# Two-stage attention and a rational feed-forward on one core: the issue order of the first thirty units taken from a table

## The chip, the cores and the metric

The kernel runs on one core of a Trainium2 chip. The metric is the device time of one execution in microseconds, the median of a few runs; lower is better. A core has five engines that run side by side, each through its own queue in order: PE (matmul), DVE, ACT and POOL (elementwise) and SP (here it only issues DMAs). An engine that waits for an instruction of another holds up everything behind it in its own queue. That is why the order matters.

## The reference

For each of 8 batches and 8 heads, 32 packed queries `p` attend to 576 keys, and the 576 queries `q` then attend to the 32 results. The 4608 x 512 output goes through a feed-forward layer of 2048 hidden columns whose activation is a ratio of polynomials.

```
p_packed = sm_attn(p, k, v)                 # sm_attn: softmax attention, scale 1/sqrt(64)
x = sm_attn(q, p_packed, p_packed)          # then heads side by side: 4608 x 512
h = x @ w_in                                # 512 -> 2048
P = a[0] + a[1]*h + a[2]*h**2 + a[3]*h**3
Q = 1 + |b[0]|*|h| + |b[1]|*h**2
out = (P / (Q + 1e-6)) @ w_out              # 2048 -> 512
```

`w_in` and `w_out` come as float64: the kernel loads their 64-bit words and converts them to float32 itself.

## The kernel before

**Tiling.** The work is cut into 128 units: batch `bb` (8), half of its 576 rows `x` (2), and chunk `c` of 256 hidden columns (8). A unit's `hidden` (L880) makes two `h` tiles of 128 x 288 on PE; ACT makes `Y`, `U` and `sq` from each; DVE multiplies `Y` up twice; POOL adds `sq` to `U`; ACT takes Ln and Exp of `U` into `V` (that is 1/Q); DVE makes two products and the result `gh`, `gl` and `G`. Three units later `acc_block` (L963) multiplies that with `w_out` into the `acc` tiles. Units 0 to 11 are plain: their matmuls take undivided float32 operands. From unit 12 on, operands are split into a high and a low part.

**Work beside the units.** `attention(bb)` (the tiles `kx`, `small`, `ppT`, `nat`, `pn`, `rv`, `AH`, `AL`) makes the attention of one batch in 16 steps during the units of the batch before; `m_chunk` (L852) folds its result with `win` into the `m` tiles. `convert` (L495) turns the 16 weight chunks into float32 while the first units run: two ACT passes, a mask and a shift on DVE (TENSOR_SCALAR, SCALAR_TENSOR_TENSOR), and a final add, on DVE (ISA in the order, CUSTOM_DVE in the profile) and POOL in turn. Its raw words lie in `m` and `w` tiles until then. `divide` (L477) later splits the converted `w_out` chunks, with an ACT cast and two POOL subtractions. `load` and `load_words` issue the DMAs, nearly all from SP.

**What sets the order.** No engine call is issued at once: `Planner` records them all, `edges` finds what depends on what, and `order` (L250) lays them out. There it runs `schedule` (L192), a list scheduler with priced instructions (`COST`, `WAY`, `DMA_RATE`), forwards and backwards for five values of `SLACK` and `ROUNDS` rounds each, and takes the layout with the earliest modelled end. `nc.pin()` (L1011) gives the first loads fixed ranks. `issue` (L281) then emits the instructions in that layout; all carry its line, L291. Where the layout leaves PE idle after the first `acc`, `idle` adds a few small matmuls on a tile of zeros.

Tile names in the order carry their buffer and a running number (`h0_5_156` is the fifth `h` tile, the first of unit 2; `V0_15` belongs to unit 14; `at0_27` and `at1_26` hold the first scores of batch 1).

## Time and profile before

| | |
|---|---|
| median of 3 runs | 777.11 us (776.41 to 777.18) |
| the profiled execution, its own time | 776.27 us |
| its span, first to last instruction | 774.5 us |
| PE / DVE / ACT / POOL busy over the span | 740.3 / 687.1 / 653.0 / 473.2 us |
| mean granted PE clock | 0.99 of full speed |

The shares over the whole span hide that the kernel has stages. Two views show them: the slices of the page, and the sums of busy time over chosen stretches, whose columns are the stretch and its length, then PE, PE's weight loads (PEld), DVE, ACT and POOL, each with its count of instructions as (x...), then the granted PE clock, the busy share of the DMA engines and GB/s. A matmul's end is modelled, so PE can read as busy while it waits; how many matmuls a stretch holds says more than its busy time. The count "idle before <-" behind a row of the timeline is how long that engine stood, and what ended it.

### The profile page before, as it was taken

The numbers are of one execution on the slowest core, as the hardware profiler recorded it, in microseconds if no ns is written. First come the engines' busy times: TensorE is split into PE (matmuls) and PEld (weight loads), VectorE is DVE, ScalarE is ACT, GpSimd is POOL, SyncE is SP. The second block draws the span as 40 slices with busy tenths as digits, with TensorE's granted clock in tenths as the row PEclk, the third lists the DMA queues.
The fourth block names the chain that finished last, engine by engine and source line by source line (L and its number), as shares of the span: only waits on it lengthen the run. The fifth ranks groups of instructions, "written<-read, shape, count | busy, mean of one in ns | idle before, by whom it ended". The sixth has DMA issues, their size and how long they took to land.

```text
span 774.5 us, 14987 instructions
## 1 busy us (share of the span) xinstructions
PE 740.3 (96%) x5332; PEld 568.4 (73%) x5332; DVE 687.1 (89%) x1289; ACT 653.0 (84%) x1465; POOL 473.2 (61%) x456
## 2 busy tenths in 40 slices
PE   2779999999999999999999999999999999999997
PEld 2445554588778887778788887778788887868885
DVE  4899999998999889998999889998999889998863
ACT  5789988999887898889886898989887898898872
POOL 1143568876695557756686556755686556866663
PEclk9879999999999999999999999999999999999999
DMA  9992630204601155023701155023701141000001
GB/s 299 338 372 76 193 41 0 85 29 55 104 1 56 44 68 91 1 87 48 111 1 55 45 55 104 2 86 41 117 1 55 42 57 35 1 2 28 28 0 41
DMA packets 152171, 56.03 MB, mean 72 GB/s; under 512 B 122272, under 2 KB 141472, under 8 KB 152096
## 3 DMA queue, kind: packets, MB, share of 16 engines
q1 hardware_dynamic: 151856, 54.81, 31.0%
q8 instruction: 42, 0.69, 0.4%
q14 instruction: 33, 0.27, 0.1%
q10 hardware_dynamic: 240, 0.26, 0.1%
HBM read 45.62 MB, written 9.44 MB: 71 GB/s over the span
## 4 chain that ended last, share of the span: by engine, by line
PE 68%; DVE 16%; DMA 7%; ACT 4%; issue 2%; POOL 2%; SPq 1%; ACTq 0%; DVEq 0%; POOLq 0%
PE acc L291 35%; PE h L291 20%; PE at L291 12%; DVE Y L291 8%; DMA w<-in_moe_w_in_dram 2%; DMA m<-in_moe_w_in_dram 2%; DVE V L291 2%; DVE kx L291 2%; DVE m L291 2%; DVE small L291 2%; DMA w<-in_q_dram 1%; SPq L291 1%; ACT Y L291 1%; POOL gl L291 1%; DVE w L291 1%
## 5 line engine op out<-in xcount | busy, mean ns | idle before, releaser
L291 POOL TENSOR_TENSOR U<-U,sq 128x576 f32<-128x576 f32 x128 | 185.4, 1449 | 94.6 <-ACT sq L291 47.3
L291 PE MATMUL acc<-w,gh 128*128 128x512 f32 x736 | 235.7, 406 | 0.7 <-DVE G L291 0.4
L291 PE MATMUL h<-AH,m 128*128 128x288 f32 x1024 | 199.5, 317 | 4.0 <-DVE Y L291 3.5
L291 PEld LDWEIGHTS h<-AH,m 128*128 128x128 f32 x1024 | 161.2, 189 | 46.5 <-DVE Y L291 24.5
L291 POOL TENSOR_TENSOR gl<-Y,gh 128x512 fp32r<-128x512 f32 x116 | 150.3, 1296 | 45.0 <-ACT gh L291 22.8
L291 PEld LDWEIGHTS acc<-w,gh 128*128 128x128 f32 x736 | 132.6, 188 | 38.7 <-issue 9.1
L291 ACT ACTIVATE Y<-h,abS 128x288 f32<-128x288 f32 x256 | 127.5, 513 | 30.5 <-PE h L291 26.2
L291 PE MATMUL acc<-w,gl 128*128 128x512 f32 x384 | 149.3, 413 | 0.0
L291 DVE SCALAR_TENSOR_TENSOR Y<-Y,abS,V 128x576 f32<-128x576 f32 x128 | 103.2, 806 | 35.2 <-ACT V L291 34.9
L291 ACT ACTIVATE sq<-h 128x288 f32<-128x288 f32 x256 | 108.4, 425 | 29.0 <-PE h L291 15.7
L291 DVE TENSOR_TENSOR Y<-Y,h 128x288 f32<-128x288 f32 x256 | 111.0, 448 | 20.6 <-ACT U L291 7.6
L291 DVE SCALAR_TENSOR_TENSOR Y<-Y,abS,h 128x288 f32<-128x288 f32 x256 | 125.7, 507 | 2.2
L291 ACT ACTIVATE U<-h 128x288 f32<-128x288 f32 x256 | 101.9, 426 | 8.0 <-DVE V L291 7.0
L291 ACT ACTIVATE V<-U,one 128x576 f32<-128x576 f32 x128 | 98.7, 771 | 8.0 <-DVE Y L291 3.8
L291 DVE SCALAR_TENSOR_TENSOR V<-U,V 128x576 f32<-128x576 f32 x128 | 96.4, 753 | 0.0
L291 PE MATMUL h<-AL,m 128*128 128x288 f32 x448 | 96.3, 295 | 0.0
L291 DVE SCALAR_TENSOR_TENSOR Y<-V,Y 128x576 f32<-128x576 f32 x116 | 87.1, 751 | 1.4
L291 PEld LDWEIGHTS acc<-w,gl 128*128 128x128 f32 x384 | 71.8, 188 | 20.7 <-issue 6.8
L291 ACT ACTIVATE V<-V 128x576 f32<-128x576 f32 x128 | 85.0, 664 | 0.8
L291 ACT CAST gh<-Y 128x512 fp32r<-128x512 f32 x116 | 74.1, 638 | 7.4 <-DVE Y L291 6.9
L291 PE MATMUL acc<-half,gh 128*128 128x512 f32 x240 | 80.0, 411 | 0.0
L291 POOL COPY G<-Y 128x64 f32<-128x64 f32 x116 | 27.5, 237 | 76.7 <-DVE Y L291 70.5
(139 smaller groups left out, 1007.5 us busy)
## 6 DMA issues: line engine op xcount, KB each, us to landing
w<-in_moe_w_out_dram SPq DMA_DIRECT2D x16, 512.0 KB, 6.6
out_dram<-half SPq DMA_DIRECT2D x15, 512.0 KB, 3.0
nat<-in_k_dram SPq DMA_DIRECT2D x48, 144.0 KB, 3.8
nat<-in_q_dram SPq DMA_DIRECT2D x48, 144.0 KB, 4.3
nat<-in_v_dram SPq DMA_DIRECT2D x24, 256.0 KB, 3.4
m<-in_moe_w_in_dram SPq DMA_DIRECT2D x10, 512.0 KB, 6.9
w<-in_moe_w_in_dram SPq DMA_DIRECT2D x6, 512.0 KB, 8.7
nat<-in_k_dram SPq DMA_DIRECT2D x4, 512.0 KB, 6.4
```

Of the source, the lines that this page charges most:

```text
L291: getattr(getattr(self.nc, engine), name)(*args, **kwargs)
```

## The change

`order` no longer schedules. It reads a permutation of all recorded instructions from a string in the source, ORDER, and emits them so. `replay` computes modelled start times for that permutation with the same prices as before; they are used only to place the small idle matmuls. The list scheduler, its slack values, and the pinning of the first loads are gone. What the permutation holds was made elsewhere: the scheduler's order, in which a search moved instructions of the first thirty units.

```diff
+ORDER = (
+    "c-rk)cXV9UnSbAC`n;Jpy-Oo$G?J`l8C>LoZ7ghDD2Bxp6TGw#5&|S_*Z?UcVY4A8gk<4lSwm=ngkmqo#s-WF;3_v<)NE-~W<1jL"
...
-    ROUNDS = 6
-    SLACK = 60, 100, 150, 220, 300
...
-    def schedule(self, before, after, rank, back=0):
...
+    def replay(self, order, before):
+
+        start, end = [0.0] * len(order), [0.0] * len(order)
+        free, port = dict(self.FIRST), {"vector": 0.0, "gpsimd": 0.0}
         mode, landed, dma = None, [], 0.0
...
+        for i in order:
+            e = self.ops[i][0]
+            s = max([free[e]] + [end[j] + self.WAY.get((self.ops[j][0], e), self.PASS) for j in before[i]])
...
+        low, high = np.frombuffer(zlib.decompress(base64.b85decode(ORDER)), np.uint8).reshape(2, -1).astype(int)
+        order = (np.cumsum(low + 256 * high) % 2**16).tolist()
...
+        self.start, self.end = self.replay(order, before)
+        self.deps, self.t0, self.best = dict(enumerate(before)), self.start, (max(self.end), self.start, self.end)
+        return order
...
-    nc.pin()
```

In the built program each engine has the same instructions as before, except that PE has 2 small idle matmuls where it had 10. From about unit 32 on, every engine's order is the same as before. (All rows of the order carry the line of `issue`, L291 before and L314 now.) Up to there most moves are short. Two places follow.

**First place: the scores of batch 1, beside units 0 to 2.** On PE, before: the scores go to `at1_26` and `at0_27`, and the last part of `at0_27` (32x64, over the remainder keys) stands behind the `h` tiles of unit 2.

```order
L291 MATMUL at1_26_173<-kx0_2_143,small_74 32x256
L291 MATMUL at0_27_174<-kx0_2_143,small_74 32x256
L291 MATMUL at1_26_173<-kx0_2_143,small_74 32x256
L291 MATMUL at0_27_174<-kx0_2_143,small_74 32x256
L291 MATMUL h0_5_156<-AH0_3_113,m1_7_135 128x288 x2
L291 MATMUL h1_6_160<-AH0_3_113,m1_7_135 128x288 x2
L291 MATMUL at0_27_174<-kx0_2_143,small_74 32x64 x4
```

On PE, now:

```order
L314 MATMUL at1_26_173<-kx0_2_143,small_74 32x256
L314 MATMUL at0_27_174<-kx0_2_143,small_74 32x256
L314 MATMUL at1_26_173<-kx0_2_143,small_74 32x256
L314 MATMUL at0_27_174<-kx0_2_143,small_74 32x256
L314 MATMUL at0_27_174<-kx0_2_143,small_74 32x64 x4
L314 MATMUL h0_5_156<-AH0_3_113,m1_7_135 128x288 x2
L314 MATMUL h1_6_160<-AH0_3_113,m1_7_135 128x288 x2
```

The remainder part of `at0_27` now stands ahead of the `h` tiles of unit 2.

On ACT at the same place, before (`at0_25` holds the transposed `p` that the scores need, `w5_7` and `m3_6` are raw weights, the `h0_5` rows are unit 2's):

```order
L291 COPY kx0_2_143<-at1_24_164 128x256
L291 COPY small_74<-at0_25_165 128x256
L291 ACTIVATE w5_7_121<-w5_7_121 128x1024
L291 ACTIVATE m3_6_134<-m3_6_134 128x1024
L291 ACTIVATE Y2_3_154<-h0_5_156,abS_68 128x288
L291 ACTIVATE U0_3_152<-h0_5_156 128x288
L291 ACTIVATE half1_2_187<-w5_7_121 128x1024
L291 ACTIVATE sq0_3_155<-h0_5_156 128x288
```

On ACT, now:

```order
L314 COPY kx0_2_143<-at1_24_164 128x256
L314 COPY small_74<-at0_25_165 128x256
L314 ACTIVATE half1_2_187<-w5_7_121 128x1024
L314 ACTIVATE w2_10_163<-w2_10_163 128x1024
L314 ACTIVATE m3_6_134<-m3_6_134 128x1024
L314 ACTIVATE sq0_3_155<-h0_5_156 128x288
L314 ACTIVATE U0_3_152<-h0_5_156 128x288
L314 ACTIVATE Y2_3_154<-h0_5_156,abS_68 128x288
```

The first pass over `w5_7` has gone from here to ten places further up, ahead of unit 1's rows; the first pass over `w2_10` has come in ahead of unit 2's; and unit 2's `Y` comes behind its `sq` and `U` instead of first.

**Second place: loads and conversion of the sixth to eighth weight chunks.** On SP, before (`w3_5`, `w4_6`, `w5_7` are raw weights, `nat1_4` keys and `AH1_2` remainder queries of batch 1):

```order
L291 DMA w2_4_118<-in_moe_w_out_dram 128x512 x2
L291 DMA pn0_2_108<-in_p_dram 32x2x64
L291 DMA nat1_4_112<-in_k_dram 128x4x256
L291 DMA AH1_2_107<-in_q_dram 32x4x128 x2
L291 DMA w3_5_119<-in_moe_w_out_dram 128x512 x2
L291 DMA pn0_2_108<-in_p_dram 32x2x64
L291 DMA w4_6_120<-in_moe_w_in_dram 128x2x256 x2
L291 DMA w5_7_121<-in_moe_w_out_dram 128x512 x2
```

On SP, now:

```order
L314 DMA w2_4_118<-in_moe_w_out_dram 128x512 x2
L314 DMA pn0_2_108<-in_p_dram 32x2x64
L314 DMA w4_6_120<-in_moe_w_in_dram 128x2x256
L314 DMA w3_5_119<-in_moe_w_out_dram 128x512 x2
L314 DMA AH1_2_107<-in_q_dram 32x4x128
L314 DMA w4_6_120<-in_moe_w_in_dram 128x2x256
L314 DMA AH1_2_107<-in_q_dram 32x4x128
L314 DMA nat1_4_112<-in_k_dram 128x4x256
L314 DMA w5_7_121<-in_moe_w_out_dram 128x512 x2
```

Half of `w4_6` and both halves of `w3_5` now go ahead of the keys `nat1_4`, which have moved behind both. Further down the queue (not shown) `w2_10` has likewise gone ahead of the values `nat0_5`, and at its start the first half of batch 0's remainder queries has gone ahead of batch 0's keys and the loads of `b` and `a` ahead of a half each of its queries.

On DVE, where batch 0's attention ends and `w2_4` and `w3_5` are converted, before:

```order
L291 TENSOR_TENSOR kx0_1_87<-kx0_1_87,small_74 128x576
L291 SCALAR_TENSOR_TENSOR w2_4_118<-w2_4_118 128x1024
L291 STREAM_TRANSPOSE AH0_3_113<-kx0_1_87 128x576
L291 TENSOR_SCALAR w3_5_119<-w3_5_119 128x1024
L291 TENSOR_TENSOR Y0_1_127<-Y0_1_127,h0_1_129 128x288
```

On DVE, now:

```order
L314 TENSOR_TENSOR kx0_1_87<-kx0_1_87,small_74 128x576
L314 STREAM_TRANSPOSE AH0_3_113<-kx0_1_87 128x576
L314 SCALAR_TENSOR_TENSOR w2_4_118<-w2_4_118 128x1024
L314 TENSOR_SCALAR w3_5_119<-w3_5_119 128x1024
L314 TENSOR_TENSOR Y0_1_127<-Y0_1_127,h1_2_132 128x288
```

The shift of `w2_4`, behind which POOL's add of `w2_4` may start, now stands behind both transpositions into `AH` and directly ahead of the mask of `w3_5`.

## Rows read from the trace of the kernel before

**Rows 1.** The page, busy tenths in 40 slices of 19.4 us.

```profile
DVE  4899999998999889998999889998999889998863
...
DMA  9992630204601155023701155023701141000001
```

**Rows 2.** Busy sums over stretches: start:end, length, engines (x instructions), clock, DMA, GB/s.

```profile
0.00:30.00 30.00, 12.80 (x171) 10.08 (x172) 16.77 (x27) 18.48 (x29) 5.79 (x9) 0.94 1.01 317
30.00:60.00 30.00, 22.66 (x183) 12.60 (x182) 27.32 (x56) 24.20 (x50) 8.32 (x5) 0.83 1.03 346
60.00:110.00 50.00, 49.34 (x326) 27.01 (x326) 49.23 (x90) 48.94 (x103) 25.37 (x14) 1.00 0.44 112
110.00:150.00 40.00, 39.74 (x207) 20.32 (x206) 39.51 (x76) 33.39 (x72) 33.08 (x27) 1.00 0.08 24
150.00:230.00 80.00, 80.00 (x602) 64.86 (x601) 73.10 (x140) 71.23 (x164) 57.74 (x58) 1.00 0.31 54
230.00:750.00 520.00, 516.23 (x3764) 417.76 (x3763) 470.75 (x888) 447.86 (x1033) 332.96 (x336) 1.00 0.25 47
```

**Rows 3.** Timeline of DVE around 60 us: start, duration, instruction, idle time before.

```profile
59.93 0.49 DVE L291 TENSOR_REDUCE small<-at 128x1 f32<-128x320 f32 x1 [2.12 <-PE at L291]
...
60.57 0.69 DVE L291 TENSOR_SCALAR w<-w 128x1024 int32<-128x1024 int32 x1
61.18 0.45 DVE L291 TENSOR_TENSOR Y<-Y,h 128x288 f32<-128x288 f32 x1
```

**Rows 4.** Timeline of PE, 55 to 60 us.

```profile
55.19 1.11 PE L291 MATMUL at<-kx,small 64*32 64x256 f32 x16 [2.07 <-ACT small L291]
56.22 3.40 PE L291 MATMUL h<-AH,m 128*128 128x288 f32 x8
59.55 0.32 PE L291 MATMUL at<-kx,small 64*32 64x64 f32 x8
```

**Rows 5.** Timeline of ACT, 42 to 59 us.

```profile
42.01 1.14 ACT L291 ACTIVATE w<-w 128x1024 f32<-128x1024 f32 x1 [1.41 <-DMA w<-in_moe_w_out_dram]
...
44.68 1.16 ACT L291 ACTIVATE w<-w 128x1024 f32<-128x1024 f32 x1 [0.44 <-DMA w<-in_moe_w_in_dram]
...
46.69 0.50 ACT L291 ACTIVATE Y<-h,abS 128x288 f32<-128x288 f32 x1
47.08 0.41 ACT L291 ACTIVATE U<-h 128x288 f32<-128x288 f32 x1
...
54.59 0.55 ACT L291 COPY small<-at 128x256 f32<-128x256 f32 x1
54.85 1.35 ACT L291 ACTIVATE w<-w 128x1024 f32<-128x1024 f32 x1
...
58.55 0.50 ACT L291 ACTIVATE Y<-h,abS 128x288 f32<-128x288 f32 x1 [1.32 <-PE h L291]
```

**Rows 6.** The chain that ended last, up to 60 us: start, length, what.

```profile
20.61 9.08 DMA w<-in_q_dram
...
47.98 8.52 DMA w<-in_moe_w_in_dram
```

**Rows 7.** Timelines of POOL and DVE: the same operations, held up and not.

```profile
44.44 2.41 POOL L291 TENSOR_TENSOR w<-w,w 128x1024 int32<-128x1024 int32 x1 [1.89 <-DVE w L291]
...
44.91 2.50 DVE L291 TENSOR_SCALAR w<-w 128x1024 int32<-128x1024 int32 x1
...
83.38 1.21 DVE L291 CUSTOM_DVE_ANT_0 win<-w,win 128x2048 uint16<-128x2048 uint16 x1
...
104.47 2.12 DVE L291 CUSTOM_DVE_ANT_0 w<-w,w 128x2048 uint16<-128x2048 uint16 x1
```

**Rows 8.** What PE's weight loads waited for, 150 to 235 us: total, times, longest.

```profile
PEld h L291 <- DVE Y L291: 1.5, 4, 0.8
PEld at L291 <- POOL half L291: 0.3, 1, 0.3
PEld acc L291 <- ACT gh L291: 0.3, 1, 0.3
```

More of the change, by code (lines that the diff above doesn't have):

```diff
@@ L1 @@
-import heapq
-from collections import deque
+import base64
+import zlib
 from contextlib import ExitStack
@@ L68, in __init__ @@
     def __init__(self, nc):
-        self.nc, self.ops, self.pinned = nc, [], 0
+        self.nc, self.ops = nc, []
     def __getattr__(self, engine):
@@ new lines, in replay @@
+    def replay(self, order, before):
+        start, end = [0.0] * len(order), [0.0] * len(order)
+        free, port = dict(self.FIRST), {"vector": 0.0, "gpsimd": 0.0}
+        mode, landed, dma = None, [], 0.0
+        for i in order:
+            e = self.ops[i][0]
+            s = max([free[e]] + [end[j] + self.WAY.get((self.ops[j][0], e), self.PASS) for j in before[i]])
+            if e == "sync" and len(landed) >= self.IN_FLIGHT:
+                s = max(s, landed[-self.IN_FLIGHT])
+            if e == "tensor" and self.modes[i] != mode:
+                s, mode = s + self.SWITCH, self.modes[i]
+            if self.shared[i]:
+                s = max(s, port["vector" if e == "gpsimd" else "gpsimd"])
+                port[e] = s + self.costs[i]
+            start[i], end[i] = s, s + self.costs[i]
+            free[e] = end[i]
+            if e == "sync":
+                dma = max(dma, s + self.DMA_START) + self.transfers[i]
+                end[i] = dma + self.DMA_END
+                landed.append(end[i])
@@ L256, in order @@
         before = self.edges()
[L257 to L279 removed]
+        low, high = np.frombuffer(zlib.decompress(base64.b85decode(ORDER)), np.uint8).reshape(2, -1).astype(int)
+        order = (np.cumsum(low + 256 * high) % 2**16).tolist()
+        place = {i: r for r, i in enumerate(order)}
+        assert sorted(order) == list(range(n)), "the order is of another program"
+        assert all(place[j] < place[i] for i in range(n) for j in before[i]), "the order breaks a dependence"
+        self.start, self.end = self.replay(order, before)
+        self.deps, self.t0, self.best = dict(enumerate(before)), self.start, (max(self.end), self.start, self.end)
+        return order
     def issue(self, idle):
```

145 lines of the change are left out of this document (71 added, 74 removed).

## The prediction

> **What bounds the kernel now.** I read the slices first [rows 1]: the DMA engines are full for the first three slices, some 60 us, and DVE is at 9 from the third to the ninth. The sums by stretch [rows 2] make stages of this. Up to 60 us the DMA share is 1.01 to 1.03, so the loads set the pace, and DVE is idle for 13.2 + 2.7 us of it. From 60 to 110 us DVE is busy 49.2 of 50 us and ACT 48.9; from 110 to 150 DVE 39.5 of 40 while ACT has 6.6 us to spare. PE reads as busy there too, but holds only 326 matmuls in 50 us and 207 in 40, that is 52 to 65 per 10 us; from 150 us on it holds 72 to 75 per 10 us and DVE falls to 73.1 of 80. So the program has three parts: loads until 60 us, DVE (for a while beside ACT) until 150, PE after that. The order behind unit 32 is unchanged, and PE has no long gap there (516 of 520 us busy). What the change brings is therefore the time by which DVE finishes its head part earlier, plus what PE's stretch from 150 to 230 us gains or loses by its own new order.
>
> **DVE's work in the head does not shrink.** I counted its queue in the two orders up to the product `V0_15` of unit 14, which runs at about 150 us: 250 instructions before, 249 now, one subtraction on 512 columns fewer; on ACT it is 247 and 247. So no large block of work is moved out of the part that DVE bounds. What can go is time in which DVE stands, or is held up: 2.7 us idle between 30 and 60 us, 0.8 between 60 and 110 and 0.5 after that [rows 2], and operations that take longer beside POOL. That is the frame: a few microseconds of 776, not tens.
>
> **Term 1, the gap ahead of 60 us.** DVE stood 2.12 us [rows 3] for a maximum over scores whose last matmuls (0.32 us) stood behind eight `h` matmuls of 3.40 us [rows 4]. Now they stand ahead of those, so this wait goes; the next one is late then. DVE's following operation of unit 2, at 61.18 [rows 3], needs an ACT pass over unit 2's first `h`. I follow that chain. ACT waited 1.41 and 0.44 us for the loads of `w3_5` and `w4_6` [rows 5], which now go earlier, and unit 0's `h`, which ACT needs next, is released 1.21 us earlier, because on DVE the last transposition now stands ahead of one such shift instead of behind it (1.21 us is the length of the byte operation of the same size in [rows 7]). So ACT is 1.85 us ahead at unit 0. It then does one more conversion pass, 1.14 us [rows 5], and ends the copy that the scores wait for at 55.14 - 1.85 + 1.14 = 54.4. The scores and their last part end 0.05 + 1.11 + 0.32 us later, at 55.9. Unit 2's first `h` reached ACT 58.55 - 56.22 = 2.33 us after its start [rows 4, 5], so now at 58.2. ACT meanwhile has three conversion passes, to 57.8, if the load of `w2_10` is there when the second begins, at 55.5. Before, its first half landed at 47.98 + 8.52 = 56.50 [rows 6]; a half is 512 KB, 1.5 us at 346 GB/s [rows 2], so it was whole at 58.0. Now it goes ahead of 512 KB of values: whole at 56.5. So ACT stands 1 us, ends the passes at 58.8, does `sq`, `U` and then `Y` in the new sequence, some 0.3 + 0.3 + 0.5 us [rows 5], and DVE can begin at 59.9 instead of 61.18. I take **-1.3 us**. The ends are 0, if ACT's pass comes no earlier, and -3.9, if all of the 2.12 us goes and with it the 1.81 us by which the mask of `w3_5` was held up (2.50 against 0.69 [rows 3, 7]).
>
> That hold-up is the one place where a page bears on the sum. The row shows the mask starting 0.47 us into POOL's add of 2.41 us and ending only after it [rows 7]. The Trainium skill, SBUF — State Buffer, section "Who interferes with whom", says that DVE in such a mode and POOL lock each other out for a whole instruction and that whichever issues first wins; the row agrees, 1.81 us of it. By that rule the new order, with the mask right behind the shift that releases POOL, gives the lock to DVE and the sum would be up to 1.8 us better, 772.1. I take nothing more for it, because behind the mask DVE waits for ACT's `Y` of unit 0 in either case, and POOL's add then ends later, which is what the first rival is about.
>
> **Term 2, work put off.** At unit 6 (about 100 us) DVE has two instructions fewer in front of it, a byte operation of 1.21 us and a mask of 0.69 [rows 3, 7], 1.9 us together, and ACT two fewer as well; by unit 14 all but the one subtraction has come back. What counts is the state at about 150 us, so I take **-0.7 us**, the price of one operation of that size (the mask of 0.69 is the nearest row), with 0 and -1.9 as ends.
>
> **Term 3, waits and hold-ups between 60 and 150 us.** DVE was idle 1.3 us there in all [rows 2], and at least one byte operation took 2.12 us for 1.21 [rows 7], 0.9 us lost to POOL. Several neighbourhoods of POOL and DVE operations are new, some of POOL's pairs of subtractions are pulled apart. I take one such hold-up less, **-0.9 us**. Ends: -3.1 (all idle time and two hold-ups gone) and +0.9 (one more).
>
> **Term 4, the first loads.** 64 KB of remainder queries now go ahead of batch 0's keys, and 3 KB of `b` and `a` ahead of its last queries. The queue is full, so they cost their bytes: 67 KB at 317 GB/s [rows 2] is **+0.2 us** on the landing that ended at 29.69 [rows 6]. Ends: 0 and +0.4.
>
> **Term 5, units 15 to 32 under PE.** Between 150 and 235 us PE's weight loads waited 2.1 us for other engines [rows 8]. The new order can take some of it or add as much. I take **-0.5 us**, ends -2.1 and +2.1. The eight small idle matmuls that go stood in gaps and cost nothing.
>
> Everything else in the table (the sequence of the two `h` tiles within a unit, of `Y`, `U` and `sq`, of the constants) I cost at nothing. What hides it is that DVE's queue is full; if the cover goes, such a swap costs one ACT pass, 0.3 to 0.5 us.
>
> **The sum.** -1.3 - 0.7 - 0.9 + 0.2 - 0.5 = -3.2 us against the profiled execution's 776.27 (span 774.5 and 1.8 us around it): 773.1. The median of the three runs, 777.11, lies 0.84 above it, so I forecast 773.9, that is 0.4% faster. The terms' ends taken together in the usual way of independent errors give 770.5 to 777. About 0.2%, 1.55 us, is what a measurement here can tell from no change: below 775.6 is faster, above 778.7 slower.
>
> **First rival: the load of `w2_10` comes late, and the gain stays inside the noise.** SP may issue it only when POOL's add has freed its buffer, which ended at 44.44 + 2.41 = 46.85 [rows 7]. If the mask of `w3_5` now goes first, POOL begins after it, at 45.6, and ends at 48.0. The first half then lands 8.52 us later [rows 6], at 56.5, the second at 58.0. ACT stands from 55.5 to 58.0, and with it unit 2's passes, which are queued behind: two passes to 60.3, `Y` at 61.4, DVE at 61.5 against 61.18. Term 1 is +0.3 then. With term 3 at nothing the sum is -0.7: 775.6, or 776.4 by the median. For it speaks that ACT waited for a load twice in just this stretch [rows 5]; against it, that the loads ahead of it in the queue are fewer now. It decides from a landing after about 57 us.
>
> **Second rival, slower: DVE behind POOL.** POOL's new order runs a subtraction, two conversion adds and unit 6's add of `U` one after another (one add is 2.41 us [rows 7]) where they stood apart, in the middle of the stretch in which DVE has no slack. Each DVE operation that shares the lock and comes second loses up to 1.8 us, as the mask did. Two more than before eat up the forecast; with three, 5.4 us, term 3 is +5.4 instead of -0.9: 776.27 - 1.3 - 0.7 + 5.4 + 0.2 - 0.5 = 779.4, by the median 780.2. For it speaks that such hold-ups are there already [rows 7]; against it, that POOL is busy only 25 of 50 us in that stretch [rows 2].
>
> **Third rival: both DVE and PE gain near their ends.** Terms 1, 3 and 5 at -2.6, -2.5 and -1.7 give -7.3 with the rest: 769.0, by the median 769.8. That the table does not do what it says I rule out: the order shows it.
>
> **How the numbers follow.** Forecast 0.54, first rival 0.24, second 0.16, third 0.06. Faster is the forecast nearly whole (0.53) and the third, 0.59; the first rival and the forecast's rest make 0.25 for no change; the second 0.16 for slower. The range reaches from the third rival's 769.8 to 779.2, which leaves out the upper two thirds of the second rival, half of the third and little else.
>
> **What would show it.** Right: no DVE wait of 2 us for PE ahead of 60 us, DVE's first operation of unit 2 at about 60 instead of 61.2, the product of unit 14 about 3 us earlier than about 150, and the same distance from there to the end but for half a microsecond. The first rival shows as an ACT wait for a load of over 2 us between 55 and 59 us. The second shows as DVE rows of 2 us and more between 80 and 150 us beside POOL's. I am wrong if unit 14 comes earlier by what I say and the end does not, for then PE's stretch is not what it seems; or if the head gains far more than DVE's idle time and hold-ups hold.

## The result and the profile after

The changed kernel is slower by a quarter of a per cent: 777.64 us against 775.95 us, medians of 22 runs each, ratio 1.0025 (95% interval 1.0015 to 1.0035). A second set of runs gave 777.46 against 775.49, ratio 1.0028 (1.0016 to 1.0040). The time lies inside the range of 769.8 to 779.2, but on the other side of no change than the forecast: the sum was -3.2 us, measured are +1.7 and +2.0. (The forecast started from the median of three runs, 777.11 us; 22 runs of the same kernel gave 775.95.) The profiled execution of the changed kernel took 778.18 us, with a span of 776.3 us.

The busy sums over the same stretches as in [rows 2], with the same columns, now read:

```profile
0.00:30.00 30.00, 12.99 (x173) 10.57 (x173) 14.62 (x34) 18.21 (x30) 6.16 (x9) 0.94 1.01 313
30.00:60.00 30.00, 18.76 (x173) 11.58 (x170) 24.51 (x45) 23.14 (x48) 9.06 (x6) 0.77 0.87 301
60.00:110.00 50.00, 49.69 (x330) 26.92 (x338) 48.34 (x93) 48.12 (x103) 20.34 (x13) 1.00 0.52 142
110.00:150.00 40.00, 40.00 (x204) 20.53 (x202) 38.59 (x78) 35.39 (x75) 33.34 (x27) 1.00 0.02 5
150.00:230.00 80.00, 79.62 (x598) 63.30 (x597) 74.30 (x140) 70.22 (x163) 56.44 (x58) 1.00 0.35 64
230.00:750.00 520.00, 515.92 (x3756) 417.81 (x3755) 469.55 (x884) 446.56 (x1031) 333.22 (x336) 1.00 0.26 47
```

Only the second row differs much. Between 30 and 60 us DVE did 45 instructions instead of 56, the DMA share fell from 1.03 to 0.87, and the granted clock of PE from 0.83 to 0.77. The DMA share is a matter of this one execution: in a second one (after_again, below) it was 1.01, and unit 2 was late all the same.

Where DVE stands is best followed by one instruction of each unit, the product that updates `V`. These are its rows for units 2, 14 and 31, first before:

```profile
70.92 0.76 DVE L291 SCALAR_TENSOR_TENSOR V<-U,V 128x576 f32<-128x576 f32 x1
...
152.00 0.76 DVE L291 SCALAR_TENSOR_TENSOR V<-U,V 128x576 f32<-128x576 f32 x1
...
244.56 0.75 DVE L291 SCALAR_TENSOR_TENSOR V<-U,V 128x576 f32<-128x576 f32 x1
```

and after:

```profile
73.17 0.76 DVE L314 SCALAR_TENSOR_TENSOR V<-U,V 128x576 f32<-128x576 f32 x1
...
151.48 0.76 DVE L314 SCALAR_TENSOR_TENSOR V<-U,V 128x576 f32<-128x576 f32 x1
...
244.90 0.75 DVE L314 SCALAR_TENSOR_TENSOR V<-U,V 128x576 f32<-128x576 f32 x1
```

The changed order is 2.25 us late at unit 2, 0.52 ahead at unit 14 and 0.34 late at unit 31. So it loses 2.25 us ahead of unit 2, gains 2.8 between units 2 and 14, as DVE's stretch should, and gives 0.9 back behind unit 14. The other 1.4 of the 1.8 us by which this execution ends later are lost at about 695 us (first experiment).

Ahead of unit 2, the timeline of DVE (as in [rows 3]) shows that the wait of 2.12 us for the scores is gone, and two others in its place:

```profile
46.24 1.96 DVE L314 TENSOR_SCALAR w<-w 128x1024 int32<-128x1024 int32 x1 [1.14 <-ACT half L314]
50.36 0.46 DVE L314 TENSOR_TENSOR Y<-Y,h 128x288 f32<-128x288 f32 x1 [2.17 <-ACT sq L314]
...
57.89 0.82 DVE L314 TENSOR_TENSOR Y<-Y,h 128x288 f32<-128x288 f32 x2 [1.60 <-ACT Y L314]
...
60.44 0.48 DVE L314 TENSOR_REDUCE small<-at 128x1 f32<-128x320 f32 x1
...
63.10 0.45 DVE L314 TENSOR_TENSOR Y<-Y,h 128x288 f32<-128x288 f32 x1
```

The last row is DVE's first operation of unit 2, at 63.10 instead of 61.18 [rows 3]. The bracket of the second row names `sq`, not `Y`: the planner lets DVE read an `h` tile in PSUM only behind everything that ACT reads from that tile (`turn` in `edges`). The timeline of ACT (compare [rows 5]):

```profile
41.25 1.13 ACT L314 ACTIVATE w<-w 128x1024 f32<-128x1024 f32 x1 [1.34 <-DMA w<-in_moe_w_out_dram]
...
43.98 1.21 ACT L314 ACTIVATE w<-w 128x1024 f32<-128x1024 f32 x1 [1.08 <-DMA w<-in_moe_w_out_dram]
...
49.13 0.90 ACT L314 ACTIVATE Y<-h,abS 128x288 f32<-128x288 f32 x2
49.91 0.42 ACT L314 ACTIVATE sq<-h 128x288 f32<-128x288 f32 x1
...
51.99 1.22 ACT L314 ACTIVATE w<-w 128x1024 f32<-128x1024 f32 x1
...
55.40 0.71 ACT L314 ACTIVATE U<-h 128x288 f32<-128x288 f32 x2 [0.69 <-PE h L314]
...
58.55 0.42 ACT L314 COPY small<-at 128x256 f32<-128x256 f32 x1
...
59.90 1.15 ACT L314 ACTIVATE w<-w 128x1024 f32<-128x1024 f32 x1
```

ACT still waited 1.34 and 1.08 us for loads. Before, it took `Y`, `U` and `sq` of one `h` tile and then of the other (the first two are in [rows 5]), so that DVE could begin with the first; now it goes to and fro between the two tiles of unit 0, and the tile that DVE wants is free only behind the `sq` that ends at 50.33. The copy that the scores need comes at 58.55 instead of 54.59. The timeline of PE (compare [rows 4]) holds the rest:

```profile
37.21 1.01 PE L314 MATMUL at<-win,ppT 64*32 64x256 f32 x16 [2.06 <-ACT m L314]
...
42.69 1.97 PE L314 MATMUL at<-ident,nat 128*128 128x128 f32 x8 [2.23 <-ACT m L314]
44.45 3.69 PE L314 MATMUL h<-AH,m 128*128 128x288 f32 x8
...
50.65 1.62 PE L314 MATMUL at<-ident,nat 128*128 128x128 f32 x8 [1.92 <-ACT m L314]
52.06 3.30 PE L314 MATMUL h<-AH,m 128*128 128x288 f32 x8
...
59.02 0.78 PE L314 MATMUL at<-kx,small 64*32 64x256 f32 x24 [3.00 <-ACT small L314]
59.92 1.24 PE L314 MATMUL h<-AH,m 128*128 128x288 f32 x4
```

Eight `h` matmuls took 3.69 and 3.30 us for units 0 and 1, and PE waited 1.9 to 3.0 us in front of them and of the scores. At full clock, four of them take 1.24 us (last row). So PE stands longer, and what it then does runs partly at the lower of its two clock levels (1.2 instead of 2.4 GHz, a granted clock of 0.50).

### The profile page after: what moved, and what is told of

The parts are those of the page before. It is cut to its first block, busy times and chain, and to the rows that moved or that the text cites. A ratio compares the mean times of both kernels' runs of the same rounds, so it can differ in the third digit from the quotient of the medians.

```text
span 776.3 us, 14959 instructions
## 1 busy us (share of the span) xinstructions
PE 738.5 (95%) x5316; PEld 568.1 (73%) x5316; DVE 681.9 (88%) x1289; ACT 652.3 (84%) x1465; POOL 469.0 (60%) x456
## 4 chain that ended last, share of the span: by engine, by line
PE 80%; ACT 6%; DVE 5%; DMA 4%; POOL 1%; issue 1%; SPq 1%; ACTq 0%; DVEq 0%; POOLq 0%
PE acc L314 41%; PE h L314 25%; PE at L314 14%; DVE Y L314 3%; DMA w<-in_moe_w_out_dram 2%; ACT Y L314 1%; DMA nat<-in_k_dram 1%; DMA m<-in_moe_w_in_dram 1%; ACT V L314 1%; DVE m L314 1%; ACT U L314 1%; ACT sq L314 1%; SPq L314 1%; POOL gl L314 1%; DVE kx L314 1%
## 5 line engine op out<-in xcount | busy, mean ns | idle before, releaser
L314 POOL TENSOR_TENSOR U<-U,sq 128x576 f32<-128x576 f32 x128 | 183.6, 1434 | 98.3 <-ACT sq L314 50.2
L314 PE MATMUL acc<-w,gh 128*128 128x512 f32 x736 | 238.0, 406 | 0.7 <-ACT half L314 0.3
L314 PE MATMUL h<-AH,m 128*128 128x288 f32 x1024 | 204.5, 318 | 3.9 <-DVE Y L314 3.8
L314 PEld LDWEIGHTS h<-AH,m 128*128 128x128 f32 x1024 | 163.8, 191 | 43.0 <-DVE Y L314 21.3
L314 POOL TENSOR_TENSOR gl<-Y,gh 128x512 fp32r<-128x512 f32 x116 | 150.2, 1295 | 49.9 <-ACT gh L314 23.2
L314 PEld LDWEIGHTS acc<-w,gh 128*128 128x128 f32 x736 | 133.1, 189 | 38.0 <-issue 8.1
L314 ACT ACTIVATE Y<-h,abS 128x288 f32<-128x288 f32 x256 | 127.4, 512 | 30.9 <-PE h L314 26.4
L314 PE MATMUL acc<-w,gl 128*128 128x512 f32 x384 | 150.1, 413 | 0.0
L314 ACT ACTIVATE sq<-h 128x288 f32<-128x288 f32 x256 | 107.4, 421 | 32.3 <-PE h L314 17.8
L314 DVE TENSOR_TENSOR Y<-Y,h 128x288 f32<-128x288 f32 x256 | 111.4, 448 | 25.6 <-ACT sq L314 9.0
L314 DVE SCALAR_TENSOR_TENSOR Y<-Y,abS,V 128x576 f32<-128x576 f32 x128 | 103.3, 807 | 34.4 <-ACT V L314 33.8
L314 DVE SCALAR_TENSOR_TENSOR Y<-Y,abS,h 128x288 f32<-128x288 f32 x256 | 126.1, 507 | 2.7
L314 ACT ACTIVATE U<-h 128x288 f32<-128x288 f32 x256 | 102.2, 424 | 8.6 <-DVE V L314 4.2
L314 ACT ACTIVATE V<-U,one 128x576 f32<-128x576 f32 x128 | 98.8, 772 | 5.8 <-DVE Y L314 3.5
L314 PE MATMUL h<-AL,m 128*128 128x288 f32 x448 | 97.8, 296 | 0.0
L314 DVE SCALAR_TENSOR_TENSOR V<-U,V 128x576 f32<-128x576 f32 x128 | 96.5, 754 | 0.0
L314 DVE SCALAR_TENSOR_TENSOR Y<-V,Y 128x576 f32<-128x576 f32 x116 | 87.2, 752 | 1.5
L314 PEld LDWEIGHTS acc<-w,gl 128*128 128x128 f32 x384 | 71.9, 188 | 22.0 <-issue 8.9
L314 ACT ACTIVATE V<-V 128x576 f32<-128x576 f32 x128 | 84.5, 660 | 1.1
L314 PE MATMUL acc<-half,gh 128*128 128x512 f32 x240 | 81.1, 412 | 0.0
L314 ACT CAST gh<-Y 128x512 fp32r<-128x512 f32 x116 | 74.0, 638 | 6.9 <-DVE Y L314 4.1
L314 PEld LDWEIGHTS h<-AL,m 128*128 128x128 f32 x448 | 73.2, 189 | 1.1
```

Of the source, the lines that this page charges most:

```text
L314: getattr(getattr(self.nc, engine), name)(*args, **kwargs)
```

## Experiments

The experiments ran in five sets, each on another chip and beside the kernel before, whose medians were 775.49, 774.66, 776.34, 775.30 and 776.13 us. So ratios are compared, and microseconds only within a set. "Half clock" is the time between 20 and 70 us at the lower clock level, twice the sum of (1 - granted clock) over stretches of 1 us. "PE waits" adds up PE's waits of over 0.15 us from 33 to 62 us. The columns for units 2, 14 and 31 give how much later (+) their product on DVE ends than in the first trace of before; they are of one execution each and hold the pace of its loads too. In the traces of after_m and after_busy_dve the first loads were late: ACT's pass that starts at 12.71 us in after_busy starts at 14.85 in after_busy_dve. The last column says whether the clock fell behind a wait at 695 us, which the first experiment is about.

| kernel | ratio to before (95%) | PE waits, us | half clock, us | unit 2 | unit 14 | unit 31 | low at 695 |
|---|---|---|---|---|---|---|---|
| before, first trace | | 7.3 | 14 | 0 | 0 | 0 | no |
| before_table | 0.9985 (0.9972 to 0.9998) | 8.2 | 7 | -2.6 | -2.6 | -2.7 | no |
| before_fill | 1.0004 (0.9990 to 1.0017) | 7.2 | 14 | -0.6 | -0.6 | -0.6 | no |
| after, first trace | 1.0025 (1.0015 to 1.0035) | 11.1 | 17 | +2.3 | -0.5 | +0.3 | yes |
| after_again | 1.0028 (1.0016 to 1.0040) | 11.7 | 17 | +1.4 | -1.4 | -0.5 | no |
| after_fill | 1.0004 (0.9987 to 1.0020) | 10.2 | 24 | +3.9 | +1.2 | +2.0 | no |
| before_busy | 1.0007 (0.9992 to 1.0023) | 3.7 | 3 | -1.9 | -1.9 | -1.8 | yes |
| after_busy | 0.9990 (0.9973 to 1.0007) | 5.0 | 3 | -2.1 | -4.8 | -3.9 | no |
| before_act74 | 1.0163 (1.0138 to 1.0187) | 9.2 | 27 | +10.0 | +10.0 | +10.0 | no |
| after_act74 | 1.0056 (1.0036 to 1.0075) | 8.4 | 17 | +3.0 | +0.3 | +1.2 | yes |
| before_m | 1.0021 (1.0004 to 1.0038) | 10.3 | 17 | +3.0 | +3.0 | +3.0 | no |
| after_m | 1.0031 (1.0016 to 1.0045) | 10.3 | 20 | +4.4 | +1.6 | +2.5 | yes |
| mix_abb | 1.0002 (0.9986 to 1.0019) | 8.8 | 14 | +0.6 | +0.6 | +0.6 | no |
| mix_bab | 1.0024 (1.0004 to 1.0044) | 9.4 | 20 | +3.4 | +3.4 | +3.3 | yes |
| mix_bba | 0.9993 (0.9976 to 1.0011) | 6.2 | 14 | +0.1 | -2.7 | -2.0 | yes |
| mix_aab | 1.0043 (1.0026 to 1.0059) | 10.7 | 17 | +2.2 | +2.2 | +2.1 | no |
| after_yfirst | 1.0016 (1.0002 to 1.0031) | 10.1 | 14 | +1.2 | -1.6 | -0.9 | yes |
| before_busy_dve | 0.9988 (0.9973 to 1.0003) | 3.7 | 3 | -1.4 | -1.4 | -1.5 | no |
| after_busy_dve | 0.9961 (0.9946 to 0.9975) | 4.5 | 3 | +0.1 | -2.7 | -1.8 | no |
| mix_bba_busy_dve | 0.9973 (0.9958 to 0.9987) | 4.8 | 3 | +0.2 | -2.5 | -1.9 | no |

### Is the loss made at 695 us or in the head?

In the first trace of the changed kernel, PE's single long wait late in the program was followed by slow matmuls. Before, then after, on PE:

```profile
694.97 0.79 PE L291 MATMUL h<-AH,m 128*128 128x288 f32 x4 [1.81 <-DVE Y L291]
```

```profile
695.63 0.90 PE L314 MATMUL h<-AH,m 128*128 128x288 f32 x4 [2.05 <-DVE Y L314]
...
696.81 1.17 PE L314 MATMUL h<-AH,m 128*128 128x288 f32 x4
```

Theory A made this the cause, theory B the head. Both orders ran a second time (`before_table` holds before's order written as a table, instruction for instruction the same program), and each with this edit, which puts twelve small matmuls on zeros ahead of the last accumulation in front of the wait:

```diff
+    FILL = 6078
...
+        if i == FILL:
+            n = 12
-        if nc.start[i] < IDLE_END and n > 0:
+        if (nc.start[i] < IDLE_END or i == FILL) and n > 0:
```

Expected of the repetition of the changed kernel:

> The changed kernel once more, unchanged, for a second trace. Theory A (the end): the head comes out about even (in the first trace unit 31's product is 0.35 us later than before) and the loss is made at about 695 us, where PE stands 2.05 us for DVE and the matmuls behind it run at a granted clock of 0.83 over 10 us. Then this trace shows the head within 0.5 us of the first one and, where the span is 776 us again, the low clock behind 695 us again. Theory B (the head): the head itself varies from execution to execution and is on average 1.5 to 2 us late. Then the product of unit 31 is late by 1.5 us or more here, and the clock behind 695 us need not fall. Time by both: 777.6, ratio 1.002 to 1.003.

Of before's order as a table:

> The order of the kernel before, written as a table and replayed; every queue holds the same instructions in the same order, with the ten idle matmuls. By both theories the time of the kernel before, ratio 0.999 to 1.001; a ratio of 1.002 would say that something other than the order differs. Its trace is the second one of the order before: by theory A the stretch behind 695 us holds the full clock in it, or where it does not, this execution is 1.4 us longer than the first one; by theory B the milestones of the head differ from the first trace's by a microsecond or more.

Of the two filled kernels:

> The changed kernel with twelve small matmuls on zeros (64x256) put into PE's queue ahead of the last accumulation before the wait at 695 us, so that PE works through most of that wait; nothing else moves. Theory A: the matmuls behind the wait keep the full clock, the stretch 690 to 700 us shows 1.00 in place of 0.83, and the time falls by 1.2 to 1.5 us to about 776.2, ratio to before 1.000 to 1.001. Theory B: the clock is a bystander, the time stays at 777.3 to 777.8, ratio 1.002 to 1.003.

> The order of the kernel before with the same twelve matmuls at the same place. Theory A: its first trace holds the full clock behind that wait, so it gains less than the changed kernel does, 0 to 0.7 us, ratio 0.999 to 1.000, and the distance between the two filled kernels is 0.3 to 0.8 us in place of 1.9. Theory B: both gain alike, or neither, and the distance between the two filled kernels stays 1.5 to 2 us.

The second trace of the changed kernel has the full clock at 695 us. Its unit 31 is 0.8 us earlier than in the first trace, where theory A had said within 0.5 us, and 0.5 us ahead of before's, where theory B had said 1.5 us late. The sums from 690 to 700 us of the first and of the second trace:

```profile
690.00:700.00 10.00, 7.95 (x49) 6.09 (x48) 9.00 (x17) 9.43 (x23) 6.01 (x7) 0.83 0.14 52
```

```profile
690.00:700.00 10.00, 7.94 (x56) 6.45 (x43) 9.27 (x17) 9.93 (x24) 6.40 (x8) 1.00 0.14 52
```

Over all traces with a wait of 1.7 us or more there, the clock fell in 7 of 15, with either order, and each time the end came 1.1 to 1.6 us later, against the first trace of before, than unit 100 had been. Where the wait was filled or shortened (five traces) it never fell. So it comes and goes, with either order: in 2 of 8 traces with before's order behind unit 2 and in 5 of 7 with the changed one, which is too few to call a difference. After_fill reads 1.0004, 0.0024 below after_again (1.9 us, give or take 1.6), and the medians of the two filled kernels lie 0.1 us apart. By the times, theory A's forecasts came in for the changed kernel, and theory B's did not. But theory A can't be the whole: unit 2 is 1.4 to 3.9 us late in all three traces of the changed order, long before 695 us, and latest in that of after_fill (an execution of 778.23 us, 2.3 above that kernel's median). So some of the loss is made at 695 us and some in the head.

The head does vary, in both orders, and with it the clock. The sums from 30 to 60 us of before_table and of after_again:

```profile
30.00:60.00 30.00, 21.72 (x183) 12.42 (x183) 29.37 (x58) 26.15 (x56) 8.38 (x6) 0.94 1.02 347
```

```profile
30.00:60.00 30.00, 18.25 (x171) 11.17 (x170) 24.64 (x46) 24.07 (x47) 9.32 (x6) 0.76 1.01 347
```

The same program as before, with a clock of 0.94 instead of 0.83, is at unit 2 2.6 us earlier, and stays so to the end. Some 1.6 us of this is the clock: the scores and the eight `h` matmuls behind them take from 55.19 to 59.62 us before [rows 4], and in before_table only from 54.14 to 56.95, the `h` matmuls 2.21 us instead of 3.40:

```profile
54.74 2.21 PE L310 MATMUL h<-AH,m 128*128 128x288 f32 x8
```

The other 1.0 us is there on ACT at 42 us already, behind a load that landed 1.0 us earlier.

A trace is one execution, but every execution has its mean granted clock, and this gives its time at half clock over the whole span (1 to 3 us at the very end included). On average it is 13.0 to 14.0 us for before (five sets), 21.7 and 20.3 for the changed kernel, and 17.3 for after_fill. So PE spends about 8 us more at the lower level with the changed order, and not only in the traces shown. Over the 22 executions of the changed kernel, each microsecond more of it goes with some 0.3 us more of time (correlation 0.74).

The repetition also says how far to trust a ratio: one program against itself gave 0.9985.

### Holding the clock in the head

Theory B2 takes the clock of the head for the cause. The edit puts 26 small matmuls into PE's waits, into an accumulator that is not in use yet; no other queue changes (in before's order the fourth group stands at 289 instead of 291):

```diff
+    BUSY = {221: 4, 239: 4, 249: 5, 291: 5, 338: 8}
...
+        if i in BUSY:
+            out = next(c[0][1][0] for _, c in nc.ops if ... tensor.name == "acc1_14_172")
+            todo = [("matmul", (out[0:D, 0:P], zero.bitcast(F32), ident), dict(start=True, stop=True))] * BUSY[i]
```

> The changed kernel with 26 small matmuls (64x128 on zeros, into an accumulator tile not yet in use) put into PE's queue ahead of the instructions for which PE waits in the head: 4 and 4 ahead of the second and third chunk of m, 5 and 5 ahead of the two transpositions of the queries, 8 ahead of batch 1's scores. Theory B2 (the clock in the head): with PE at work in its waits the granted clock of 36 to 60 us, 0.72 to 0.75 in three traces of this order, rises to 0.85 or more, the eight h matmuls of units 0 and 1 take 2.2 us in place of 3.3 to 3.7, and the time falls by 1 to 2 us to 775.6 to 776.6, ratio 1.000 to 1.0015. Theory A2: the waits for ACT set the pace there and not the clock; PE's matmuls get shorter but wait for the same copies, the time falls by under 0.6 us, ratio 1.002 or more. If the filling lengthens PE's queue instead, the time rises by up to 1 us.

> The order of before with the same 26 small matmuls at the same instructions. Theory B2: its head had a granted clock of 0.83 and 0.94 in two traces over 30 to 60 us, so it can gain less: 0 to 1.2 us, ratio 0.9985 to 1.000, and its trace shows 0.90 or more over that stretch. Theory A2: no change within 0.5 us, ratio 0.9995 to 1.0005.

The changed order now takes 774.36 us against 774.66 for before. The ratio falls from 1.0028 to 0.9990, that is 2.9 us, give or take 1.6. PE's timeline of after_busy, against the one above (the `zero` row is the filling):

```profile
48.73 2.11 PE L311 MATMUL h<-AH,m 128*128 128x288 f32 x8
...
51.42 1.96 PE L308 MATMUL acc<-ident,zero 128*64 128x128 f32 x16
54.69 0.78 PE L311 MATMUL at<-kx,small 64*32 64x256 f32 x24 [1.31 <-ACT small L311]
```

Unit 1's eight `h` matmuls take 2.11 us instead of 3.30, the scores start at 54.69 instead of 59.02. The sums from 30 to 60 us of after_busy and of before_busy:

```profile
30.00:60.00 30.00, 24.91 (x230) 16.39 (x229) 26.00 (x49) 25.96 (x53) 9.35 (x6) 0.94 1.02 350
```

```profile
30.00:60.00 30.00, 26.27 (x241) 16.88 (x241) 29.15 (x60) 25.96 (x54) 8.60 (x5) 1.00 1.06 349
```

Nothing but PE's idle time was touched, so these 2.9 us were the clock's: theory B2 holds for the changed order. Theory A2 had allowed 0.6. Over all executions the time at half clock fell to 7.9 us. For before's order B2 had forecast 0.9985 to 1.000, and it gained nothing that could be measured by the same filling (1.0007), although its time at half clock fell as well, from 13.3 us to 6.4; in its trace the head is 1.9 us ahead at unit 2, and 1.5 us of that is lost again at 695 us. So a microsecond at half clock costs the changed order more than it costs before's; why is not shown.

The change also took out eight of the ten small idle matmuls. They are not the cause: in the trace of before all ten stand between 66 and 119 us, where the granted clock is 1.00 with either order, and mix_aab (below), which has all ten, is 2.2 us late at unit 2 like the changed kernel.

### Which instructions make PE stand longer?

Theory A2 looked to ACT's order alone. First, all but two of ACT's first 74 instructions were exchanged between the orders. An excerpt (the changed kernel, 33 to 37 us):

```diff
-ACTIVATE w2_4_118<-w2_4_118 128x1024
-COPY m0_5_122<-at0_13_124 128x256
 COPY m0_5_122<-at1_12_123 128x256
+COPY m0_5_122<-at0_13_124 128x256
+ACTIVATE w2_4_118<-w2_4_118 128x1024
```

> The changed kernel, but ACT's first 74 instructions (all up to the copy of the small tile for batch 1's scores, some 55 to 59 us) in the sequence of before, except for two one-column steps of the constants that stay early because DVE's new order needs them. The other queues stay as changed. Theory A2 (ACT's order in the head): in the changed kernel, conversion passes that wait for loads stand ahead of the copies of the m tiles, and the U and sq steps of units 0 and 1 ahead of Y, so PE waits 2.1 to 3.8 us for m at 37 us, 2.2 for m at 42, 3.0 for small at 56 to 59, and DVE 2.2 to 2.9 us for Y at 49. With the old sequence these go back to below 2.1 us and the time falls by 1.3 to 2 us to 775.5 to 776.2, ratio 0.999 to 1.001. Theory C (the clock by chance, whatever the order): the granted clock of the head falls in some executions and not in others, ACT's sequence has no say in it, and the time stays at 777 to 777.6, ratio 1.002 to 1.003.

> The reverse: the kernel before with ACT's same 72 instructions in the changed sequence. Theory A2: it takes on the waits of the changed kernel, without what the other queues gain by their new order: 1.5 to 3 us slower than before, 777 to 778.5, ratio 1.002 to 1.004. Theory C: no change, ratio 0.999 to 1.001.

Both came out slower than what they started from. The exchange reached back to the first loads, where the raw chunks `m0` and `m1` change places on ACT but not on DVE and SP, and batch 0's attention itself was late by about 3 us. So these two say nothing on the place in question, only that ACT's order is tied to the other queues. The next pair exchanged thirteen instructions, from 33 to 45 us:

> The changed kernel, but thirteen ACT instructions between 33 and 45 us (the copies of the m chunks 0 to 2, two exponentials of batch 0 and the conversion passes of w2_4, w3_5 and w4_6) in the sequence of before, copies ahead of passes; all else as changed. This cuts the swap of 74 down to the place where the changed kernel's PE waits begin. Theory D (the trigger is here): the waits of PE for m ahead of the second and third chunk and the transposition, 5.1 to 6.0 us together in the changed kernel, come back to the 2.7 to 4.4 us of before, the granted clock of 36 to 60 us rises from 0.74 to 0.85 or more, and the time falls by 1 to 2 us to 775.6 to 776.6, ratio 1.000 to 1.0015. Theory E (the trigger is elsewhere, in the Y, U and sq sequence of units 0 and 1 or in PE's own order): no change, 777 to 777.8, ratio 1.002 to 1.003.

> The kernel before with the same thirteen ACT instructions in the changed sequence, passes ahead of copies. Theory D: PE's waits for m grow by 1.5 to 3 us, the clock of 36 to 60 us falls below 0.8, and the time rises by 1 to 3 us, ratio 1.0015 to 1.004. Theory E: ratio 0.999 to 1.001.

Before's order suffers by it as theory D says (1.0021, PE's waits from 7.3 to 10.3 us, half clock 17 us). But giving the changed order before's sequence there didn't help (1.0031), although its waits ahead of the second and third chunk of `m` and the transposition fell to 0.50, 1.21 and 2.24 us. Theory D is not the answer for the changed kernel; in its trace PE's chain was already 1.3 us later at 36 us (its first loads were late), and the clock fell for longer (20 us).

So I cut all five queues at two points where both orders have issued the same set of instructions, and took each third whole: up to unit 0's `h` (some 42 us), to unit 2's `h` and the scores of batch 1 (some 58 us), and the rest. The letters name the thirds: a is the changed order, b before's.

> Before's order, except that on all five queues the first third (all up to the h matmuls of unit 0, some 42 us) has the changed order; the small idle matmuls as before. Theory F (the loss is made here, by the m copies behind conversion passes and the new load order): PE waits for m as in the changed kernel, the half-clock time between 20 and 70 us goes to 8.5 us or more, and the time rises by 1.5 to 3 us, ratio 1.002 to 1.004. Theory G (it is made in the second third): ratio 0.999 to 1.001.

> Before's order, except that the second third (from unit 0's h to unit 2's h and the scores of batch 1, some 42 to 58 us) has the changed order. Theory G (Y behind U and sq on ACT, the small copy late, one conversion pass more ahead of it): PE waits 3 us for small and DVE 2 us and more for Y, the time rises by 1 to 2 us, ratio 1.001 to 1.003. Theory F: ratio 0.998 to 1.0005, the latter if the tail of the scores ahead of unit 2's h gains its 2 us wait on DVE.

> Before's order up to unit 2's h and the scores (some 58 us) and the changed order from there on. Theory H (the gain lies here: at a held clock the changed order gets ahead between units 2 and 14 by some 3 us and keeps 1.4): the head keeps before's clock, and the time falls by 1 to 2 us, ratio 0.9975 to 0.999. If the gain lay in the first two thirds, ratio 0.9995 to 1.0015.

> The complement: the changed order up to some 58 us, before's from there on. Theory H with either F or G: it takes the loss without the gain, 1 to 2 us slower than the changed kernel, ratio to before 1.003 to 1.005. If the gain lay in the first two thirds, it is as the changed kernel or faster, ratio 1.001 to 1.0025.

Theory F falls and G's place holds: the first third alone costs nothing that can be measured (1.0002), the second carries the loss (1.0024, and 1.0043 with the first). The intervals of the two thirds alone overlap; what is clear of them is the second third on top of the first, 1.0043 against 1.0002. The time at half clock, averaged over all executions, points the same way: 14.5 us in mix_abb, 15.3 in mix_bba, 17.7 in mix_bab, 19.6 in mix_aab. The last third is where the order gains, as theory H says: 2.7 to 2.8 us from unit 2 to 14 wherever it is in (after, after_again, after_fill, after_busy, mix_bba), nothing where it is not. Of this mix_bba shows only 0.9993 in its time; its trace has one of the falls at 695 us. Mix_bab has DVE's wait for ACT and PE's for the small copy in before's surroundings:

```profile
49.20 0.46 DVE L310 TENSOR_TENSOR Y<-Y,h 128x288 f32<-128x288 f32 x1 [1.94 <-ACT sq L310]
```

```profile
57.85 1.32 PE L310 MATMUL at<-kx,small 64*32 64x256 f32 x24 [3.00 <-ACT small L310]
```

Half clock takes 20 us in its trace (an execution of 780.89 us, 3.3 above that kernel's median), 14 in those of mix_abb and mix_bba. The last test gave ACT a sequence of its own in that third, `Y` first, the pass of `w5_7` behind the small copy:

```diff
-ACTIVATE sq0_1_128<-h0_1_129 128x288
-ACTIVATE U0_1_125<-h0_1_129 128x288
-ACTIVATE U0_1_125<-h1_2_132 128x288
-COPY m1_7_135<-at0_21_151 128x256
 ACTIVATE Y0_1_127<-h1_2_132,abS_68 128x288
 ACTIVATE Y0_1_127<-h0_1_129,abS_68 128x288
...
+COPY m1_7_135<-at0_21_151 128x256
...
-ACTIVATE w5_7_121<-w5_7_121 128x1024
...
+ACTIVATE w5_7_121<-w5_7_121 128x1024
```

> The changed kernel, with the 24 ACT instructions of the second third (units 0 and 1 and the copies beside them) in a new sequence that follows the changed order's own h tiles: Y of both h tiles first, then U and sq, and the pass of w5_7 behind the small copy. Theory G (Y last and the extra pass are the cause): DVE's waits for Y, 2.2 to 2.9 and 1.6 us, fall below 1 us, PE's wait for small from 3.0 to 3.2 us to about 2.0, the half-clock loss over 20 to 70 us from 8.5 us to 7 or less, and the time falls by 1 to 2 us to 775.5 to 776.5, ratio 1.000 to 1.0015. If the loss hangs on PE's or DVE's own new order there, the time stays within 0.6 us of the changed kernel, ratio 1.002 to 1.003.

The ratio of 1.0016 can't be told from the changed kernel's 1.0025. PE's wait for the small copy fell from 3.0 to 2.25 us, but DVE's wait did not fall (2.17 and 2.92 us in the first two traces of the changed kernel), and the time at half clock over all executions stayed at 19.9 us. Its row on DVE:

```profile
48.61 0.45 DVE L311 TENSOR_TENSOR Y<-Y,h 128x288 f32<-128x288 f32 x1 [3.09 <-ACT sq L311]
```

and ACT's at that place:

```profile
46.79 0.89 ACT L311 ACTIVATE Y<-h,abS 128x288 f32<-128x288 f32 x2 [1.82 <-PE h L311]
47.57 0.71 ACT L311 ACTIVATE U<-h 128x288 f32<-128x288 f32 x2
48.15 0.73 ACT L311 ACTIVATE sq<-h 128x288 f32<-128x288 f32 x2
```

`Y` was there at about 47.3 and DVE began at 48.61, right behind the first `sq`. So theory G named the wrong thing: what counts is when the third reader of one tile is done, and my sequence went to and fro between the tiles just like the changed one. A sequence that finishes one tile first, as before's does, was not tried in the changed order. That this is the main cause in the second third is read from the rows and not shown by a run.

### The version that beats both

PE's wait at 695 us comes from DVE: two subtractions for an `m` chunk stand between the products on the `h` tile that PE waits for. They were moved behind:

```diff
-TENSOR_TENSOR m3_37_1402<-at0_195_1403,m3_37_1402 128x512
...
-TENSOR_TENSOR m3_37_1402<-at1_196_1404,m3_37_1402 128x512
...
+TENSOR_TENSOR m3_37_1402<-at0_195_1403,m3_37_1402 128x512
+TENSOR_TENSOR m3_37_1402<-at1_196_1404,m3_37_1402 128x512
```

> The changed order with the 26 small matmuls in the head, and on DVE two subtractions of an m chunk that stand at 692 us between the products of two units moved behind the four products on the h tiles, of which the first releases the h tile that PE waits for 1.8 to 2.05 us at 695 us. Both remaining stretches of half clock (head, and behind 695 us) should be gone: granted clock 0.996 or more, the wait at 695 us 0.6 to 1.0 us, the time 0.8 to 1.8 us below the same kernel without the move: 772.6 to 773.6, ratio 0.9965 to 0.998. If the wait at 695 us is kept by another engine, the time stays at 774.4.

> The order of before with the same two edits, the 26 matmuls and the two subtractions moved. With the clock held in both, the distance to its partner is what the new order is worth by itself. Theory B2 says 1.3 to 2.1 us (at unit 31 the filled traces stand 1.3 to 2.1 us apart): this kernel 774.2 to 775.4, ratio 0.9985 to 1.0. If the new order is worth nothing, the two agree within 0.5 us.

> What helped, joined: before's order up to some 58 us, the changed order from there on, the 26 small matmuls in PE's waits of the head and the two subtractions on DVE moved at 692 us. If the gain of the last third and the held clock add up: as fast as the changed order with both edits or up to 1 us faster, 772.8 to 774, ratio 0.995 to 0.9975. If the second third of the changed order is worth something by itself once the clock is held, this one is slower than that: 774 to 775, ratio 0.9975 to 0.999.

In after_busy_dve the wait is down to

```profile
692.58 0.80 PE L311 MATMUL h<-AH,m 128*128 128x288 f32 x4 [1.12 <-DVE Y L311]
```

and the time is 773.79 us, ratio 0.9961 (0.9946 to 0.9975): faster than both kernels. With the clock held at both places, the changed order is worth 773.79 against 775.23, 1.4 us in its favour. Taking before's first two thirds instead brought nothing more (774.08, ratio 0.9973): once the clock is held, no cost of the second third is left that could be measured.

The ratios side by side:

| | nothing filled | filled at 695 us | filled in the head | filled in the head, wait at 695 us cut |
|---|---|---|---|---|
| before's order | 1 (its copy 0.9985) | 1.0004 | 1.0007 | 0.9988 |
| the changed order | 1.0025 and 1.0028 | 1.0004 | 0.9990 | 0.9961 |

In the changed order either edit takes off about as much as the whole loss, and both together more. In before's order none of the edits is clear of the noise.

## Why the prediction was wrong

**The step that failed is term 1.** It follows a chain of ACT and PE instructions to DVE's first operation of unit 2 at 59.9; it came at 63.10. Three links broke. ACT's waits for loads did not go: 1.34 and 1.08 us instead of 1.41 and 0.44 [rows 5]. The sequence of `Y`, `U` and `sq`, which I costed at nothing because DVE's queue would cover it, was not covered: DVE waited 2.17 and 1.60 us, since ACT finished neither tile early. And I kept the duration of every PE group. The signs were in the rows: [rows 2] has a granted clock of 0.83 for 30 to 60 us and 1.00 behind, and eight `h` matmuls take 3.40 us [rows 4], where after_busy needs 2.11. I read PE as an engine that waits there anyway, and didn't ask what longer waits do to the pace of what follows. The sum had no term for the clock.

The hold-up of the mask of `w3_5`, which I took nothing for, went both ways. In the first trace the mask stood 1.14 us for ACT's second pass, POOL's add had begun at 45.23, and it took 1.96 us (first row of DVE above). In after_again it came right behind the shift, 0.2 us ahead of POOL's add:

```profile
45.38 0.69 DVE L314 TENSOR_SCALAR w<-w 128x1024 int32<-128x1024 int32 x1
```

It brought nothing, for the reason I gave: DVE then waited for ACT, 2.92 us.

**What it should have held.** At unit 2 the three unfilled traces of before's whole order stand at 0, -2.6 and -0.6 us, those of the changed order at 2.3, 1.4 and 3.9. The means differ by 3.6 us against the change. With PE kept busy (two traces each) they differ by 0.7: by -0.2 in one set and by +1.6 in the other, where the changed order's first loads were late. So, as an estimate from ten traces that lie up to 2.6 us apart within one order, the clock takes about 2.9 of the 3.6 us, and the new waits by themselves 0.7, where I had -1.3.

**Terms 2 and 3 were right in kind and too small.** Together I had -1.6 from unit 2 to 14; it was -2.7 to -2.8 in every trace with this part of the order. In the first traces DVE's busy time there fell by 4.5 us (79.85 to 75.36), and its idle time grew from 1.2 to 3.0 us. DVE has 143 instructions there instead of 145. Four held-up byte operations of 1.53, 1.64, 2.12 and 2.12 us (one is in [rows 7]) are gone; at 1.21 us each, as not held up [rows 7], that is 2.6 us. Three operations on `small` tiles, of 0.62, 1.03 and 1.19 us before, take under 0.2 us each now; what had held those is not shown. So the hold-ups went the other way than the second rival said, and no DVE operation there reaches 2 us.

**Term 4** could not be seen: the traces of one program differ by more than its 0.2 us.

**Term 5 had the wrong sign.** From unit 14 to 31 the changed order gives back 0.8 to 0.9 us (0.6 to 0.7 in mix_bba, mix_bba_busy_dve and after_yfirst). PE's weight loads from 150 to 235 us now wait for other engines like this, the columns as in [rows 8]:

```profile
PEld acc L314 <- ACT gh L314: 1.8, 6, 0.4
PEld h L314 <- DVE Y L314: 0.9, 4, 0.3
PEld acc L314 <- ACT U L314: 0.8, 1, 0.8
```

With 2.5 us in smaller ones that is 6.0 us against 2.1 [rows 8].

**The whole, as measured:** +3.6 for the head, -2.75 for DVE's stretch, +0.9 under PE is +1.7 us; the medians say +1.7 and +2.0. That they agree so well is partly luck: the sum leaves out what is lost at 695 us, some 0.4 us more for the changed order in the same six traces (one fall in six), and by the times of the filled kernels it may be more. That the time came to lie in the range is luck too; no rival held the mechanism. The first rival's, a late load of `w2_10`, was not there: ACT's pass on it at 59.90 (last row of ACT above) didn't wait. The terms' ends, added as independent errors, give 770.0 to 777.4 rather than 770.5 to 777, which changes nothing. The test I had set, that I am wrong if unit 14 comes earlier and the end does not, applied: unit 14 came 0.5 us earlier in the first trace, and the end 1.8 us later.

## What to carry to other kernels

A search over an issue order that prices every instruction at a fixed duration can't see that an engine's pace depends on how busy it is: ahead of the first steady stretch, count PE's waits in the old and the new order as a cost of their own, and read the granted clock there first. A cheap test tells whether such a loss is the clock's or the order's: a few matmuls on zeros in the waits, nothing else moved. Queues that were laid out together can't be mixed one by one; cut all of them at points where both orders have issued the same set.

## What was unexpected of the hardware

PE's clock fell to its lower level in the head although no single wait of PE there was longer than 2.1 us from 33 to 62 us in the first trace of before, and at 695 us behind a wait of 1.7 to 2.1 us after hundreds of microseconds at full clock, in 7 of 15 executions. Each fall cost the end 1.1 to 1.6 us there. The Trainium skill, TensorE: Matmul & The Clock Gate, section "Part 1: The HAM clock gate", says that the low clock is the resting state and that activity lifts it. The runs agree: with 26 matmuls on zeros in the waits, the time at half clock between 20 and 70 us fell from 17 us to 3, and the changed kernel's time by 2.9 us (in before's order from 14 us to 3, without a gain that could be measured).

One program and its exact copy came out at a ratio of 0.9985 with an interval that leaves out 1, and in their first traces the heads differed by 2.6 us, 1.6 of it through the clock. A difference of 0.15% between two orders of this kernel should not be trusted from one set of runs; the 0.25% of the changed kernel came out in two.
